# Spreading a row of 1/sigma over the partitions: three products with the identity in place of a round trip through DRAM

## The chip, the cores and the metric

The kernel runs on one core of one Trainium2 chip. The metric is the device time of one execution in microseconds (us). A core has five engines, each with its own instruction queue that is worked off in order: TensorE (PE in the profile; its weight loads stand apart as PEld), VectorE (DVE), ScalarE (ACT), GpSimd (POOL) and SyncE (SP), which here only issues transfers. ACT and POOL issue transfers too; a queue's own issuing instructions are marked SPq and ACTq.

## The reference

Three parts follow each other. Attention over short windows gives x of shape 4 x 768 x 512. A Fourier mixer adds to x the real part of its two-dimensional Fourier transform, normalises each position, applies a two-layer network and adds the result. A gated convolutional network ends it.

```python
u = x + real(fft(fft(x, axis=1), axis=2))
mu = mean(u, axis=-1); var = mean((u - mu) ** 2, axis=-1)
un = (u - mu) / sqrt(var + 1e-06)
x2 = u + maximum(un @ w_ch1, 0) @ w_ch2          # 512 -> 2048 -> 512
h = maximum(x2 @ w_in, 0)                        # 512 -> 1024
...
out = (h * sigmoid(conv(h)) @ w_out)
```

## The kernel before

Positions lie along the free dimension and features on the partitions. The 4 x 768 positions are cut into 8 chunks of 384 (`TC`); chunk c is half of batch c // 2. Each fp32 number is held as a high and a low part in the type fp32r, and a product of two of them is three matmuls (`split3`, recorded on line 65 by `accumulate`).

The mixer's network is computed on u - mu without the division. Since relu(a x) = a relu(x) for positive a, the factor 1/sigma of a position may be multiplied in at the end. That is what the tile `rb` is for: it holds the 384 values of 1/sigma of one chunk on each of the 128 partitions.

The network has 16 tiles f of 128 hidden features. The first 4 are done early, in `dense`. The rest is done in 13 steps s, which one loop walks through. A step is one chunk with a run of tiles f: steps 0 to 4 take tiles 4 to 8 of chunks 0 to 4, steps 5 to 9 take tiles 9 to 15 of the same chunks (7 tiles), steps 10 to 12 take tiles 4 to 15 of chunks 5 to 7 (12 tiles). The eight steps from 5 on are the last of their chunk, and each of these runs `prep_stat` once. For each tile the loop calls:

- `g1`: 12 matmuls into the PSUM tile `h`; ACT makes `hh` of it (line 477) and DVE `hl` (line 478);
- one piece of `prep_stat`, up to its next `yield`, as long as there is one;
- `g2`: 12 matmuls of an earlier tile into four accumulators `acc`. At the last tile of a step `finish` follows: DVE adds `acc` to `yp` (line 709), multiplies by `rb` (line 715), and POOL's queue adds the result into `ucd` in DRAM (line 716). This comes in the first tile of the next step.

The pieces of `prep_stat`, with the tile j of the step in which each is called: j = 0, ACT squares u (line 662) and POOL's queue adds the mean into DRAM; j = 1, DVE sums the squares into `sq` (lines 666 and 667); j = 2, nothing; j = 3, PE sums over the partitions into `pvar` (line 672: three fp32 matmuls with one column, which the profile counts as six), and DVE and ACT read it into `st`; j = 4, DVE makes 1/sigma in `st` (lines 678 to 682), as 128 partitions x 3 values; j = 5, ACT's queue writes those 384 values to `rd` in DRAM (line 684); j = 6, SP's queue reads the row back, once for each partition, into `rb` (line 687).

The order of the work on each engine is that of the code. PSUM tiles `h`, `pvar` and whatever else is tagged "g" take turns in three buffers here. The same loop runs the decoding of the weights of the last part (tiles `w`, `wsc`, `wlb`, `whb`, `wo`, `wihd`) on ACT, DVE and SP's queue, in pieces.

Of the kernel before, what the change touches and what calls it, by code (L numbers as in the profile page):

```python
# [7 lines left out]
F32 = mybir.dt.float32  # L8
# [8 lines left out]
NB, NH, S, HD = 4, 8, 768, 64  # L17
# [8 lines left out]
TC = 384  # L26
# [19 lines left out]
def fourier_mixer_kernel(ctx: ExitStack, tc: tile.TileContext, qk, vw, w1, w2, w_in, w_out, conv_w,  # L46
                         mask, ident, dtab, orow, stab, sgn, out):
    nc = tc.nc
    mm = nc.tensor.matmul

    dram = ctx.enter_context(tc.tile_pool(name="dram", bufs=1, space=DRAM))
# [15 lines left out]
    const = ctx.enter_context(tc.tile_pool(name="const", bufs=1))  # L67
# [5 lines left out]
    nc.vector.memset(expb, -float(EXP0 << 23))  # L73
    expl = const.tile([128, 1], F32, name="expl")
    nc.vector.memset(expl, -float(896 << 23))
    stg = ctx.enter_context(tc.tile_pool(name="stg", bufs=2))
    rx = ctx.enter_context(tc.tile_pool(name="rx", bufs=1, side="right"))
    a1p = tc.alloc_tile_pool(name="a1p", bufs=2)
    ps_g = tc.alloc_tile_pool(name="ps_g", bufs=PSG, space=PSUM)
# [3 lines left out]
    order = []  # L83
    for f in range(NI, NF1):
        order += [("1", f), ("2", f)]
    rd = [dram.tile([1, TC], F32, name=f"rd{c}") for c in range(2 * NB)]
    wihd = [dram.tile([128, 1024], F32, name=f"wihd{f}") for f in range(NF2)]
    wohd = [dram.tile([128, 1024], F32, name=f"wohd{f}") for f in range(NF2)]

# [88 lines left out]
    for nm, dst in (("a", w1h), ("b", w1l), ("c", w2h), ("d", w2l)):  # L178
        t = rx.tile([128, 512 * NI], F32R, tag=f"rx{nm}", name=f"rx{nm}")
# [8 lines left out]
    cst = tc.alloc_tile_pool(name="cst", bufs=1)  # L188
# [5 lines left out]
    ps_o = tc.alloc_tile_pool(name="ps_o", bufs=1, space=PSUM)  # L194

    mask_sb = cst.tile([QB, 3, KW], F32, name="mask_sb")
    ident_sb = cst.tile([128, 128], F32, name="ident_sb")
    dtab_sb = cst.tile([128, 2, 2, CW + SW], F32R, name="dtab_sb")
    orow_sb = cst.tile([1, CW], F32R, name="orow_sb")
    stab_sb = cst.tile([97, 2, 8, 194], F32R, name="stab_sb")  # L200
# [367 lines left out]
    with tc.manual_schedule():  # L568
# [44 lines left out]
        ps_g = tc.alloc_tile_pool(name="ps_g2", bufs=3, space=PSUM, reuse_waits="tile")  # L613
        uc1 = tc.alloc_tile_pool(name="uc1", bufs=1, reuse_waits="tile")
        NC1 = NB * S // TC
        NTC = TC // 128
# [5 lines left out]
        def half(c):  # L622
            b, hf = divmod(c, 2)
            return b, slice(hf * TC, hf * TC + TC)
# [30 lines left out]
        def prep_stat(s):  # L655

            d = ck[s]
            c = steps[s][0]
            b, ss = half(c)
            sq = uc1.tile([128, 4, TC], F32, tag="sq", name="sq")  # L660
            for j in (0, 2):
                nc.scalar.activation(out=sq[:, j:j + 2], in_=d["us"][:, j:j + 2], func=AF.Square)
            nc.gpsimd.dma_start(out=ucd[b][:, :, ss], accum_op=ALU.add,
                                in_=mud[b][:, ss].rearrange("o (k t) -> o k t", k=1).to_broadcast([128, 4, TC]))
            yield
            nc.vector.tensor_tensor(out=sq[:, 0:2], in0=sq[:, 0:2], in1=sq[:, 2:4], op=ALU.add)  # L666
            nc.vector.tensor_tensor(out=sq[:, 0], in0=sq[:, 0], in1=sq[:, 1], op=ALU.add)
            yield
            yield
            p = ps_g.tile([128, 512], F32, tag="g", name="pvar")  # L670
            for t in range(NTC):
                mm(p[:, t:t + 1], sq[:, 0, t * 128:t * 128 + 128], onesm[:, 0:1], start=True, stop=True)  # L672
            st = uc1.tile([128, 4, NTC], F32, tag="st", name="st", bufs=2)
            ve, sd, r, e = (st[:, i] for i in range(4))
            nc.vector.tensor_scalar(out=ve, in0=p[:, 0:NTC], scalar1=0.5, scalar2=1e-6, op0=ALU.mult, op1=ALU.add)
            nc.scalar.activation(out=sd, in_=p[:, 0:NTC], func=AF.Sqrt, bias=epsc[:, 0:1], scale=0.5)
            yield
            nc.vector.reciprocal(out=r, in_=sd)
            nc.vector.tensor_tensor(out=e, in0=r, in1=r, op=ALU.mult)
            nc.vector.tensor_tensor(out=e, in0=e, in1=ve, op=ALU.mult)  # L680
            nc.vector.tensor_scalar(out=e, in0=e, scalar1=-0.5, scalar2=1.5, op0=ALU.mult, op1=ALU.add)
            nc.vector.tensor_tensor(out=r, in0=r, in1=e, op=ALU.mult)
            yield
            nc.scalar.dma_start(out=rd[c].rearrange("o (t p) -> p (o t)", p=128), in_=r)
            d["r"] = a1p.tile([128, TC], F32, tag="y", name="rb")
            yield
            nc.sync.dma_start(out=d["r"], in_=rd[c].to_broadcast([128, TC]))

        def g2(s, f):
            d = ck[s]  # L690
# [40 lines left out]
        for i, (s, f) in enumerate(seq):  # L731
            c, fs, last = steps[s]
# [9 lines left out]
            if j == 0 and last:  # L742
                stat = prep_stat(s)
# [106 lines left out]
    with tc.manual_schedule():  # L850
# [21 lines left out]
        for i in range(len(steps) + LAG):  # L872
# [5 lines left out]
            if i < len(steps):  # L878
                b, f = steps[i]
# [132 lines left out]
```

## Time and profile before

| | |
|---|---|
| time, median of 3 runs (lowest to highest) | 1075.61 us (1075.1 to 1075.64) |
| the profiled execution's own time | 1073.26 us |
| its span, first to last instruction | 1071.5 us |
| PE busy | 1024.6 us (96%) |
| DVE busy | 662.2 us (62%) |
| ACT busy | 431.4 us (40%) |
| mean granted clock of PE | 0.973 |
| steps 5 to 12 of the loop, about | 470 to 796 us of the span |

The profiled execution lies 2.35 us under the median, and the span 1.76 us under that execution's own time. A busy PE counts its time at any clock, so 96% isn't the share in which it works at its full rate; the granted clock says how far the rate fell.

### The profile page before, as it was taken

The numbers are of one execution on the slowest core, as the hardware profiler recorded it, in microseconds if no ns is written. First come the engines' busy times: TensorE is split into PE (matmuls) and PEld (weight loads), VectorE is DVE, ScalarE is ACT, GpSimd is POOL, SyncE is SP. The second block draws the span as 40 slices with busy tenths as digits, with TensorE's granted clock in tenths as the row PEclk, the third lists the DMA queues.
The fourth block names the chain that finished last, engine by engine and source line by source line (L and its number), as shares of the span: only waits on it lengthen the run. The fifth ranks groups of instructions, "written<-read, shape, count | busy, mean of one in ns | idle before, by whom it ended". The sixth has DMA issues, their size and how long they took to land.

```text
span 1071.5 us, 16522 instructions
## 1 busy us (share of the span) xinstructions
PE 1024.6 (96%) x6352; PEld 974.1 (91%) x6352; DVE 662.2 (62%) x1505; ACT 431.4 (40%) x894; POOL 229.9 (21%) x236
## 2 busy tenths in 40 slices
PE   6879999899998999999989998999999999999998
PEld 5769998799998999999989998999998999999997
DVE  5897659865989666664654544342337656566554
ACT  6855446653343433233322231222126445454442
POOL 2353343652513000010000000000202322222222
PEclk9877999899999999999989998999999999999999
DMA  7841433520435544587798689461945302010001
GB/s 248 281 137 56 144 106 107 178 56 31 141 108 192 197 152 153 200 187 129 183 206 173 115 157 193 120 96 37 207 111 139 103 12 82 26 59 1 33 27 60
DMA packets 68127, 132.44 MB, mean 124 GB/s; under 512 B 8215, under 2 KB 43519, under 8 KB 67823
## 3 DMA queue, kind: packets, MB, share of 16 engines
q1 hardware_dynamic: 52576, 103.93, 31.6%
q0 software_dynamic: 12016, 27.16, 14.4%
q10 hardware_dynamic: 3456, 0.29, 0.3%
q8 instruction: 50, 0.82, 0.3%
q14 instruction: 29, 0.24, 0.1%
HBM read 93.85 MB, written 43.80 MB: 128 GB/s over the span
## 4 chain that ended last, share of the span: by engine, by line
PE 57%; DMA 8%; DVE 4%; issue 1%; ACT 0%; POOL 0%; DVEq 0%; ACTq 0%; POOLq 0%; SPq 0%
PE acc L65 27%; PE h L65 16%; PE ph L65 11%; DMA rd<-st 5%; DMA rb<-rd 2%; PE y L65 2%; DVE yp L715 1%; DMA wot<-wohd 1%; PE pvar L672 1%; DMA ucd<-uc 0%; DVE wsc L135 0%; DVE sq L666 0%; DVE hl L478 0%; DVE whb L131 0%; DVE uc L165 0%
## 5 line engine op out<-in xcount | busy, mean ns | idle before, releaser
L65 PE MATMUL acc<-hh,w 128*128 128x384 f32 x768 | 214.7, 343 | 0.0
L65 PE MATMUL h<-uh,w 128*128 128x384 f32 x768 | 212.0, 340 | 0.0
L478 DVE SCALAR_TENSOR_TENSOR hl<-h,hh 128x384 fp32r<-128x384 f32 x128 | 70.6, 555 | 190.1 <-ACT hh L477 189.1
L477 ACT ACTIVATE hh<-h 128x384 fp32r<-128x384 f32 x128 | 61.9, 488 | 234.0 <-PE h L65 233.9
L65 PEld LDWEIGHTS acc<-hh,w 128*128 128x128 f32 x768 | 143.7, 192 | 0.0
L65 PEld LDWEIGHTS h<-uh,w 128*128 128x128 f32 x768 | 142.7, 191 | 0.0
L65 PE MATMUL ph<-xh,wit 128*128 128x384 f32 x512 | 136.3, 337 | 2.2 <-ACT hrow L802 2.2
L65 PE MATMUL acc<-hl,w 128*128 128x384 f32 x384 | 131.6, 343 | 0.0
L65 PE MATMUL h<-ul,w 128*128 128x384 f32 x384 | 130.4, 340 | 0.0
L65 PE MATMUL acc<-wot,hgh 128*128 128x512 f32 x384 | 119.7, 393 | 0.0
L810 DVE SCALAR_TENSOR_TENSOR cv<-hrow,cw_sb,cv 128x768 f32<-128x768 f32 x64 | 110.1, 1720 | 3.1 <-ACT cv L804 2.0
L822 POOL TENSOR_TENSOR hgl<-cv,hgh 128x768 fp32r<-128x768 f32 x32 | 60.3, 1883 | 196.1 <-ACT hgh L821 180.5
L65 PEld LDWEIGHTS ph<-xh,wit 128*128 128x128 f32 x512 | 93.3, 188 | 4.0 <-ACT hrow L802 2.8
L816 DVE TENSOR_TENSOR cv<-hrow,cv 128x768 f32<-128x768 f32 x32 | 30.7, 960 | 99.0 <-ACT cv L815 98.9
L65 PE MATMUL ph<-xl,wit 128*128 128x384 f32 x256 | 86.1, 336 | 0.0
L65 PEld LDWEIGHTS acc<-wot,hgh 128*128 128x128 f32 x384 | 71.7, 188 | 13.4
L241 ACT ACTIVATE sm<-sm,ngm 96x128 f32<-96x128 f32 x256 | 80.0, 392 | 7.7 <-DVE ngm L233 7.7
L65 PE MATMUL acc<-wot,hgl 128*128 128x512 f32 x192 | 74.7, 389 | 0.0
L65 PEld LDWEIGHTS acc<-hl,w 128*128 128x128 f32 x384 | 73.7, 192 | 0.0
L65 PEld LDWEIGHTS h<-ul,w 128*128 128x128 f32 x384 | 73.3, 191 | 0.0
L802 ACT ACTIVATE hrow<-ph 128x384 f32<-128x384 f32 x64 | 31.2, 493 | 102.2 <-PE ph L65 101.1
L716 POOL DMA_DIRECT2D ucd<-yp x8 | 9.7, 1208 | 286.3 <-DVE yp L715 194.4
(142 smaller groups left out, 1912.1 us busy)
## 6 DMA issues: line engine op xcount, KB each, us to landing
w<-in_w SPq DMA_DIRECT2D x32, 512.0 KB, 4.1
qk<-in_qk SPq DMA_DIRECT2D x32, 448.0 KB, 3.6
us<-ucd SPq DMA_DIRECT2D x13, 768.0 KB, 7.3
yp<-yd SPq DMA_DIRECT2D x13, 768.0 KB, 7.9
vw<-in_vw SPq DMA_DIRECT2D x32, 260.0 KB, 2.7
ucd<-uc SPq DMA_DIRECT2D x8, 768.0 KB, 3.8
yd<-y SPq DMA_DIRECT2D x32, 192.0 KB, 1.9
ucd<-mud POOLq DMA_DIRECT2D x8, 768.0 KB, 20.2
```

Of the source, the lines that this page charges most:

```text
L65: mm(o, a, b, start=(start and i == 0), stop=(stop and i == n - 1))
L241: nc.scalar.activation(out=d["ex"][:, h, :], in_=d["ex"][:, h, :], func=AF.Exp, scale=-1.0, bias=d["ngm"][:, h:h + 1])
L477: nc.scalar.activation(out=hh, in_=p[:, 0:TC], func=AF.Relu)
L478: nc.vector.scalar_tensor_tensor(out=hl, in0=p[:, 0:TC], scalar=0.0, in1=hh.bitcast(F32), op0=ALU.max, op1=ALU.subtract)
L672: mm(p[:, t:t + 1], sq[:, 0, t * 128:t * 128 + 128], onesm[:, 0:1], start=True, stop=True)
L715: nc.vector.tensor_tensor(out=y[:, t:t + 2], in0=y[:, t:t + 2], in1=bc, op=ALU.mult)
L716: nc.gpsimd.dma_start(out=ucd[b][:, :, ss], in_=y, accum_op=ALU.add)
L802: nc.scalar.activation(out=h[:, 1 + hf * TC:1 + hf * TC + TC], in_=p[:, 0:TC], func=AF.Relu)
L810: nc.vector.scalar_tensor_tensor(out=cv, in0=h[:, j:j + S], scalar=cw_sb[:, j, f:f + 1], in1=cv, op0=ALU.mult, op1=ALU.add)
L816: nc.vector.tensor_tensor(out=cv, in0=h[:, 1:S + 1], in1=cv, op=ALU.mult)
L822: nc.gpsimd.tensor_tensor(out=hgl[i], in0=cv, in1=hgh[i].bitcast(F32), op=ALU.subtract)
```

## The change

The row no longer goes to DRAM. At j = 5 PE makes three products, one for each 128 positions: the weights are one column of 1/sigma, repeated 128 times, and the moving operand is the 128 x 128 identity, so that each of the 128 partitions of the result gets the 128 values. ACT copies the result from PSUM into `rb`. The write to `rd` (ACT's queue), the read (SP's queue) and the piece at j = 6 go. The identity, which only the attention part used before, moves into a pool that lives to the end. That takes 512 bytes of each partition, and what lies behind it in SBUF moves up by as much.

```diff
+    ident_sb = const.tile([128, 128], F32, name="ident_sb")
...
-    rd = [dram.tile([1, TC], F32, name=f"rd{c}") for c in range(2 * NB)]
...
-    ident_sb = cst.tile([128, 128], F32, name="ident_sb")
...
             nc.vector.tensor_tensor(out=r, in0=r, in1=e, op=ALU.mult)
             yield
-            nc.scalar.dma_start(out=rd[c].rearrange("o (t p) -> p (o t)", p=128), in_=r)
+            p = ps_g.tile([128, 512], F32, tag="g", name="prow")
+            for t in range(NTC):
+                mm(p[:, t * 128:t * 128 + 128], r[:, t:t + 1].to_broadcast([128, 128]), ident_sb, start=True, stop=True)
             d["r"] = a1p.tile([128, TC], F32, tag="y", name="rb")
-            yield
-            nc.sync.dma_start(out=d["r"], in_=rd[c].to_broadcast([128, TC]))
+            nc.scalar.copy(d["r"], p[:, 0:TC])
```

On PE, at j = 5 of step 6 (chunk 1), these rows stood between the products of `h` and of `acc` before (the numbers behind the names are buffers):

```order
L65 MATMUL h<-uh,w_14_4389 128x384 x2
L65 MATMUL h<-ul,w_14_4389 128x384
L65 MATMUL h<-uh,w_14_4389 128x384
L65 MATMUL acc<-hh,w_12_4386 128x384 [waits Activation_49]
L65 MATMUL acc<-hl,w_12_4386 128x384
L65 MATMUL acc<-hh,w_12_4386 128x384 x2
```

and these now:

```order
L65 MATMUL h<-uh,w_14_4381 128x384 x2
L65 MATMUL h<-ul,w_14_4381 128x384
L65 MATMUL h<-uh,w_14_4381 128x384
L685 MATMUL prow<-ident_sb,st 128x128 [waits DVE_49,Activation_49]
L685 MATMUL prow<-ident_sb,st 128x128 x2
L65 MATMUL acc<-hh,w_12_4378 128x384
L65 MATMUL acc<-hl,w_12_4378 128x384
```

Three products came in, and the first waits for DVE (the values) and for ACT (the PSUM buffer, and with it `hh`, for which `acc` waited before).

On ACT, in the same place, the queue held before:

```order
L477 ACTIVATE hh<-h 128x384 [waits PE_49,Activation_49] x2
L684 DMA rd_93<-st 128x3x1 [waits DMAHW2_49,DVE_49]
L162 CAST uh<-us 128x768 [waits DMAHW5_49]
L162 CAST uh<-us 128x768
L134 COPY wo<-whb 128x512 [waits DMAHW3_49,DVE_49]
```

and now:

```order
L476 ACTIVATE hh<-h 128x384 [waits PE_49,Activation_49] x2
L687 COPY rb<-prow 128x384 [waits PE_49]
L162 CAST uh<-us 128x768 [waits DMAHW3_49]
L162 CAST uh<-us 128x768
L134 COPY wo<-whb 128x512 [waits DMAHW1_49,DVE_49]
```

A copy that waits for PE stands where the write was issued. On SP, at j = 6 of the same step, one issue before left between a spill of decoded weights and a fetch of the next; before:

```order
L144 DMA wihd_103<-wo 128x512 [waits DMAHW1_49,DVE_49]
L687 DMA rb<-rd_93 128x384 [waits DMAHW3_49,DMAHW2_49]
L94 DMA w_6224<-in_w_in 128x512 [waits DMAHW4_49,DVE_49]
L143 DMA wihd_104<-wo 128x512 [waits DMAHW5_49,Activation_49]
L144 DMA wihd_104<-wo 128x512 [waits DMAHW6_49,DVE_49]
L630 DMA us<-ucd_58 128x4x384 [waits DMAHW7_49]
```

and now:

```order
L144 DMA wihd_96<-wo 128x512 [waits DMAHW7_49,DVE_49]
L94 DMA w_6222<-in_w_in 128x512 [waits DMAHW0_49,DVE_49]
L143 DMA wihd_97<-wo 128x512 [waits DMAHW1_49,Activation_49]
L144 DMA wihd_97<-wo 128x512 [waits DMAHW2_49,DVE_49]
L629 DMA us<-ucd_58 128x4x384 [waits DMAHW3_49]
```

Here the read of the row, which waited for its own write, is gone, and nothing else has moved. On the other queues the order of the instructions is the same as before.

## Rows read from the trace of the kernel before

**Rows 1.** The page, busy time: us, share of the span, instructions.

```profile
PE 1024.6 (96%) x6352; PEld 974.1 (91%) x6352; DVE 662.2 (62%) x1505; ACT 431.4 (40%) x894; POOL 229.9 (21%) x236
```

**Rows 2.** Who PE waited for, 300 to 830 us: us in total, times, longest.

```profile
PE pvar L672 <- DVE sq L667: 10.5, 4, 4.1
```

**Rows 3.** PE's `pvar` products in time: start, us, engine, line [idle before].

```profile
482.75 0.72 PE L672 MATMUL pvar<-onesm,sq 128*128 128x1 f32 x6
...
513.13 0.74 PEld L672 LDWEIGHTS pvar<-onesm,sq 128*128 128x128 f32 x6 [0.29 <-DVE sq L667]
...
546.35 1.44 PE L672 MATMUL pvar<-onesm,sq 128*128 128x1 f32 x6 [2.72 <-DVE sq L667]
...
582.04 0.83 PE L672 MATMUL pvar<-onesm,sq 128*128 128x1 f32 x6 [2.25 <-DVE sq L667]
...
615.49 0.83 PE L672 MATMUL pvar<-onesm,sq 128*128 128x1 f32 x6 [1.48 <-DVE sq L667]
...
651.47 1.18 PE L672 MATMUL pvar<-onesm,sq 128*128 128x1 f32 x6 [4.09 <-DVE sq L667]
...
705.86 0.72 PE L672 MATMUL pvar<-onesm,sq 128*128 128x1 f32 x6
...
756.99 0.72 PE L672 MATMUL pvar<-onesm,sq 128*128 128x1 f32 x6
```

**Rows 4.** Stretches: span, busy of PE, PEld, DVE, ACT, POOL, PEclk, DMA share, GB/s.

```profile
480.00:513.00 33.00, 33.00 (x191) 32.83 (x189) 18.78 (x39) 11.49 (x19) 1.21 (x1) 1.00 0.81 179
...
546.00:582.00 36.00, 33.44 (x174) 33.12 (x174) 17.48 (x37) 9.00 (x16) 3.42 (x3) 0.91 0.89 166
...
706.00:757.00 51.00, 51.00 (x296) 51.00 (x295) 14.35 (x28) 9.08 (x17) 2.87 (x4) 1.00 0.37 61
```

**Rows 5.** DVE in time, from the end of step 6 on.

```profile
534.17 1.94 DVE L709 TENSOR_TENSOR yp<-acc,yp 128x384 f32<-128x384 f32 x4
541.34 1.83 DVE L715 TENSOR_TENSOR yp<-yp,rb 128x768 f32<-128x768 f32 x2 [5.24 <-DMA rb<-rd]
...
544.29 0.55 DVE L478 SCALAR_TENSOR_TENSOR hl<-h,hh 128x384 fp32r<-128x384 f32 x1
544.76 0.94 DVE L666 TENSOR_TENSOR sq<-sq 128x768 f32<-128x768 f32 x1
545.74 0.56 DVE L667 TENSOR_TENSOR sq<-sq 128x384 f32<-128x384 f32 x1
```

**Rows 6.** Who DVE waited for: us in total, times, longest.

```profile
DVE yp L715 <- DMA rb<-rd: 25.6, 5, 7.4
```

**Rows 7.** The row's way in step 6: last DVE instruction, write and read issued.

```profile
520.19 0.16 DVE L682 TENSOR_TENSOR st<-st 128x3 f32<-128x3 f32 x1
...
522.69 0.37 ACTq L684 DMA_DIRECT2D rd<-st  x1
...
536.14 0.32 SPq L687 DMA_DIRECT2D rb<-rd  x1
```

**Rows 8.** PE in time: an fp32 product of 384 columns, and what follows.

```profile
315.98 0.81 PE L410 MATMUL pm<-gs,onesm 128*128 128x384 f32 x2
316.33 0.66 PE L65 MATMUL p<-stab_sb,zh 96*128 96x194 f32 x2
316.83 0.27 PE L65 MATMUL p<-stab_sb,zl 96*128 96x194 f32 x1
316.94 0.39 PE L65 MATMUL p<-stab_sb,zh 96*128 96x194 f32 x2
```

**Rows 9.** PE in time, behind the `pvar` of 705.86.

```profile
706.44 0.42 PE L65 MATMUL acc<-hh,w 128*128 128x384 f32 x1
706.70 0.34 PE L65 MATMUL acc<-hl,w 128*128 128x384 f32 x1
706.88 0.51 PE L65 MATMUL acc<-hh,w 128*128 128x384 f32 x2
```

**Rows 10.** ACT: a copy of 128 x 384 from PSUM.

```profile
20.21 0.48 ACT L162 COPY at<-atp 128x384 f32<-128x384 f32 x1 [0.23 <-PE atp L250]
```

## Prediction

> **What bounds the kernel now.** The page's busy table comes first: PE is busy for 1024.6 us of a span of 1071.5 [rows 1]. So PE is the path, and a change elsewhere pays only where it ends one of PE's waits or takes work from it. The list of who waited for whom, cut to 300 to 830 us (the loop over the 13 steps), shows one wait that counts: `pvar`, for the sum of squares `sq` from DVE [rows 2]. The same products in order of time show where: five of the eight `pvar` come late, with idle times of 0.29, 2.72, 2.25, 1.48 and 4.09 us, together 10.83 us [rows 3]. (The list counts four of them and a little less, since PE's weight load waits apart.)
>
> Idle time is not the whole price. A stretch without a stall, 706 to 757 us, has a granted clock of 1.00; the one that holds the end of one stall and the beginning of the next, 546 to 582 us, has 0.91 [rows 4]. So PE falls from the upper level of 2.4 GHz to the lower one, 1.2 GHz, for some microseconds after a stall. The whole price can be read from the distances between the starts of `pvar`, since the work between them is fixed: seven tiles up to step 10, twelve after it. Without a stall twelve tiles take 756.99 - 705.86 = 51.13 us. Seven take 513.13 - 482.75 = 30.38 us, of which 0.29 is idle, so 30.09. (The two fit: five tiles more cost 21.04 us, 4.21 each.) The others, start to start, are 33.22, 35.69, 33.45, 35.98 and, with twelve tiles, 54.39 us [rows 3]. Over the unstalled length they lose 3.13, 5.60, 3.36, 5.89 and 3.26 us; with the first 0.29 that is **21.5 us**, about half idle and half lower clock.
>
> Why is `sq` late? DVE's timeline at the end of step 6 shows it. DVE has added the accumulators by 536.1 us and then stands still for 5.24 us, until `rb` has landed; only then come the multiplication, some decoding, `hl` and the two sums into `sq`, which end at 546.3 [rows 5]. PE starts `pvar` at 546.35 [rows 3]. Over the whole run DVE waited five times for `rb`, 25.6 us in all [rows 6], once for each stall. And `rb` is late because of its way: 1/sigma is there at about 520.4, the write is issued at 522.69, and the read, which waits for the write, only at 536.14 [rows 7].
>
> **What the change takes away.** Everything between 522.7 us and the landing before 541.34 goes. The products stand where the write was issued, so in this step `rb` would be ready about 1.5 us after 522.5 us, and DVE asks for it at 536.1: 12 us of cover. Then the multiplication and all behind it come 5.24 us earlier, and `sq` is ready 5.24 - 2.72 = 2.5 us before PE asks. At the longest wait it is 7.4 - 4.09 = 3.3 us, and over the five (25.6 - 10.83) / 5 = 3.0 us on average. So each of the five stalls should go whole, and with it the fall of the clock behind it, since it needs the stall. Next in line for PE would be `hl`, which the same queue delivers, also 5 us earlier. I take the full 21.5 us; the lower end is given by the second rival.
>
> A rule in the Trainium skill speaks against this: the page DMA: Bandwidth & Descriptors (section Anatomy of one DMA, SWDGE path) puts the fixed cost of a transfer at about 2 us. By it the row would be written and back about 4.5 us after 522.69 (an estimate: twice 2 us and 0.45 us for 197 KB), at 527.2, long before DVE asks, and the change would take away nothing. The trace differs: between the two issues alone lie 13.45 us [rows 7]. The measurement decides; what it leaves of that case is the fourth rival.
>
> **What it adds on PE.** Eight times three fp32 products of 128 columns, six passes in the profile's count, as `pvar` has. No row shows this form, so it is bounded. From below: `pvar` itself, six loads of 128 x 128 weights with one column each. From its start at 705.86 to the next product 0.58 us pass, 0.097 a pass, all of it weight load; the first product behind takes 0.26 instead of 0.18 [rows 3, 9]. So the detour costs 0.66 us, and eight cost 5.3 us. The columns: the fp32 product `pm` with 384 columns and the two short products behind it take 0.85 us from 315.98 to 316.83; the short ones take 0.11 each [rows 8], which leaves 0.63 for two passes and, by thirds, 0.105 us for 128 columns. If loads lie under the columns of the pass before, as `pvar`'s neighbours do, a pass costs the larger of the two: 6 x 0.105 + 0.08 = 0.71. I take **0.75**, in all **6.0 us**. From above: if nothing overlaps, 6 x 0.202 + 0.08 = 1.29, in all 10.3 us. That the weights are one column read 128 times has no row at all; I leave it inside these bounds, which would still hold a load twice as long.
>
> The page TensorE: Matmul & The Clock Gate (section LDWEIGHTS) makes a load as long as its columns, 107 ns for 128. The trace has 97 ns for it. By the page's figure a detour would be 6 x 0.107 + 0.08 = 0.72 us (an estimate), 5.8 us in all.
>
> The first of the new products waits for DVE's 1/sigma and for a PSUM buffer. The values end at 520.35, and ACT's issue behind `hh`, which marks the end of `h` on PE, stands at 522.69 [rows 7]: a slack of about 2.2 us. The seven other steps repeat this pair within 0.4 us. The buffer was `pvar`'s, read two tiles before.
>
> **What it moves.** ACT loses an issue of 0.37 us and gains a copy of about 0.48 [rows 7, 10]. Behind it the two casts of `uh` wait for it, and behind those `hh` of the next tile, whose products end 4.2 us and a detour later; ACT is busy for 9.00 of 36 us there [rows 4]. It costs nothing; without that cover it would be 8 x 0.5 us. SP's queue no longer stands before the read, so fetches, `us` and `yp` go out earlier; they are wanted many microseconds later. The transfer engines are busy for 0.81 of a stretch that PE runs through without a stall, and 0.89 of a stalled one [rows 4]. With the steps shorter, the same bytes come in less time, but 8 x 197 KB of reads go. The 512 bytes that shift later tiles change which old tile a new one waits for; those waits are for work done long before. Both at nothing.
>
> **The sum.** -21.5 + 6.0 = -15.5 us. On the profiled execution's own time, 1073.26, that gives 1057.8. The median of the runs shown is 2.35 us above it; on 1075.61 it gives **1060.1 us**.
>
> **The rivals.**
> 1. *The products are dear.* Loads of a repeated column don't overlap with the columns, or are slower. Against it: weight loads and matmuls are both busy nearly all the time in the same stretches [rows 4]. -21.5 + 10.3 = -11.2, 1064.4 us.
> 2. *Another wait takes the place of the one removed.* With the row out of the way, DVE is held by something else in the same place, say a fetch of weights in transfer engines that are fuller, so that `sq` still comes late in about half the cases. For it: 0.89 of DMA share. Against it: 2.5 to 3.3 us of margin. -10.8 + 6.0 = -4.8, 1070.8 us.
> 3. *Slower: PE waits for 1/sigma.* The new products stand in PE's queue, in front of `acc`; the DMA waited elsewhere. If DVE delivers the values more than 2.2 us later than now, PE stalls in eight places instead of five. The stalls of 1.48 to 4.09 us cost 3.1 to 5.9 with the clock. It decides from (21.5 - 6.0) / 8 = 1.9 us for each place; at 3 us each the kernel is 8.5 us slower, 1084.1. Against it: DVE makes these values right behind `hl`, and a DVE that waits less is earlier, not later.
> 4. *Nothing is gained.* `rb` has long landed, and DVE's wait is only put down to it and ends with something else; then only the products are left, +6.0, 1081.6 us. Against it: the five waits of rows 6 and the read's issue 5.2 us before the end of the one shown [rows 5, 7]. (This is where the rule of DMA: Bandwidth & Descriptors in the Trainium skill leads.)
>
> That the change doesn't do what it says is no rival: the order of the instructions shows the products on PE and no transfer.
>
> **Chances and range.** The forecast 0.74, dear products 0.12, a new wait 0.08, PE waits for 1/sigma 0.04, nothing gained 0.02. About 0.2% (2.1 us) is what a measurement of this kernel can tell from no change. The first three are faster, less 0.01 for a new wait that eats nearly all: faster 0.93, same 0.02 (with as much from a milder third rival), slower 0.05. The range: the cheapest products give 1075.6 - 21.5 + 5.3 = 1059.4, and as the runs shown lie up to 2.4 us beside the profiled one, 1057.0; the dearest give 1064.4, and with 2.4 us again 1066.8. The rivals beyond it hold 0.14.
>
> **What the profile after would show.** DVE's wait for `rb` gone, and line 715's multiplication right behind the additions. No idle time before `pvar`, starts 30.8 us apart over seven tiles (30.09 and a detour of 0.75) and 51.9 over twelve, with a granted clock of 1.00 from 480 to 790 us. Six passes of `prow` in 0.6 to 0.8 us, eight times, without idle time before them. The forecast is wrong if `pvar` still waits, if `prow` waits for DVE, or if its passes take 0.2 us each.

## The result and the profile after

The changed kernel takes **1060.8 us** (median of 4 runs, 1059.1 to 1064.62) against 1075.62 us before (4 runs, 1075.1 to 1076.58): a ratio of **0.9866, interval 0.9839 to 0.9894**. The profiled execution took 1059.1 us with a span of 1057.3; before it was 1073.26 and 1071.5. The medians here take in every execution, while the ratios and intervals are of the means and leave out the few executions that ran more than 1.5% over the fastest of their kernel.

The page's busy times of the changed kernel come first, beside [rows 1]:

```profile
PE 1023.2 (97%) x6400; PEld 974.5 (92%) x6400; DVE 662.5 (63%) x1505; ACT 435.4 (41%) x902; POOL 230.0 (22%) x236
```

PE has 48 instructions more, eight times six passes, and was still busy for no longer. Between the first and the last `pvar` it was busy for 263.75 us before, at a granted clock of 0.96, and for 258.00 us now, at 1.00: matmuls that no longer ran at the lower clock gave back more than the passes took. ACT's eight more are the copies. The list of who PE waited for, from 300 to 830 us, beside [rows 2] (us in total, times, longest), is now:

```profile
PE ph L65 <- ACT hrow L802: 2.2, 2, 1.8
PE h L65 <- DVE y L160: 1.6, 1, 1.6
PE y L65 <- DVE hl L477: 1.3, 2, 0.8
```

`pvar`, with 10.5 us the largest before, is not in it. The eight `pvar` products in order of time, beside [rows 3] (start, us), have no idle time in brackets any more:

```profile
484.51 0.72 PE L671 MATMUL pvar<-onesm,sq 128*128 128x1 f32 x6
515.41 0.72 PE L671 MATMUL pvar<-onesm,sq 128*128 128x1 f32 x6
546.31 0.72 PE L671 MATMUL pvar<-onesm,sq 128*128 128x1 f32 x6
...
638.86 0.72 PE L671 MATMUL pvar<-onesm,sq 128*128 128x1 f32 x6
690.69 0.72 PE L671 MATMUL pvar<-onesm,sq 128*128 128x1 f32 x6
742.49 0.72 PE L671 MATMUL pvar<-onesm,sq 128*128 128x1 f32 x6
```

They are 30.90 us apart over seven tiles (30.74 up to step 10) and 51.8 over twelve; 30.8 and 51.9 were predicted. The first lies 1.76 us later than before, and the span behind the last is 0.3 us longer, so the whole difference of the spans (14.2 us) and a little more arises between the first and the last: 274.24 us before, 257.98 now, 16.26 less.

The stretches, beside [rows 4] (span, busy of PE, PEld, DVE, ACT, POOL, granted clock, DMA share, GB/s):

```profile
480.00:790.00 310.00, 309.64 (x1799) 309.32 (x1798) 146.62 (x298) 84.32 (x152) 22.46 (x27) 1.00 0.64 149
546.00:577.00 31.00, 31.00 (x182) 31.00 (x181) 17.29 (x36) 9.48 (x17) 2.42 (x2) 1.00 0.87 177
```

The clock is 1.00 over the whole loop, and PE is busy without a gap. DVE in order of time at the end of step 6 shows what [rows 5] showed:

```profile
537.01 1.94 DVE L709 TENSOR_TENSOR yp<-acc,yp 128x384 f32<-128x384 f32 x4
538.87 1.82 DVE L715 TENSOR_TENSOR yp<-yp,rb 128x768 f32<-128x768 f32 x2
...
542.27 0.95 DVE L665 TENSOR_TENSOR sq<-sq 128x768 f32<-128x768 f32 x1
543.26 0.56 DVE L666 TENSOR_TENSOR sq<-sq 128x384 f32<-128x384 f32 x1
```

The multiplication stands right behind the additions. `sq` ends at 543.82, and PE asks for it at 546.31: 2.5 us of margin. Of the row's own way, the last DVE instruction on 1/sigma [rows 7] and the copy that replaced the transfers [rows 10] are these, in order of time:

```profile
522.36 0.16 DVE L681 TENSOR_TENSOR st<-st 128x3 f32<-128x3 f32 x1
...
525.39 0.48 ACT L687 COPY rb<-prow 128x384 f32<-128x384 f32 x1
```

And PE's products between them, with their neighbours, beside [rows 8, 9]:

```profile
524.52 0.83 PE L685 MATMUL prow<-ident_sb,st 128*128 128x128 f32 x6
525.11 0.42 PE L65 MATMUL acc<-hh,w 128*128 128x384 f32 x1
525.37 0.34 PE L65 MATMUL acc<-hl,w 128*128 128x384 f32 x1
525.54 0.52 PE L65 MATMUL acc<-hh,w 128*128 128x384 f32 x2
```

`rb` is there at 525.9, 13 us before DVE uses it. The six passes hold the next product back by 0.59 us, and the one behind starts after 0.26 instead of 0.18: a detour of 0.67 us, which is `pvar`'s 0.66 [rows 3, 9]. Divided by six, 0.59 us is 0.098 a pass, but that is not a pass's own length: taken one by one, the passes start 0.11 us apart (524.52, 524.63, 524.74, 524.86, 524.97, 525.08), and only behind the last one the next product follows after 0.03.

### The profile page after: what moved, and what is told of

It is laid out like the page before. It is cut to its first block, busy times and chain, and to the rows that moved or that the text cites. A ratio compares the mean times of both kernels' runs of the same rounds, so it can differ in the third digit from the quotient of the medians.

```text
span 1057.3 us, 16601 instructions
## 1 busy us (share of the span) xinstructions
PE 1023.2 (97%) x6400; PEld 974.5 (92%) x6400; DVE 662.5 (63%) x1505; ACT 435.4 (41%) x902; POOL 230.0 (22%) x236
## 4 chain that ended last, share of the span: by engine, by line
PE 65%; DVE 2%; DMA 1%; issue 0%; ACT 0%; POOL 0%; DVEq 0%; POOLq 0%; SPq 0%
PE acc L65 31%; PE h L65 20%; PE ph L65 12%; PE y L65 2%; DMA wot<-wohd 1%; PE prow L685 1%; PE pvar L671 0%; DMA ucd<-uc 0%; DVE wsc L135 0%; DVE uc L165 0%; DVE yp L709 0%; DMA out<-o 0%; DVE yp L715 0%; DVE hl L477 0%; DVE w L139 0%
## 5 line engine op out<-in xcount | busy, mean ns | idle before, releaser
L65 PE MATMUL acc<-hh,w 128*128 128x384 f32 x768 | 211.2, 338 | 0.0
L65 PE MATMUL h<-uh,w 128*128 128x384 f32 x768 | 209.7, 337 | 0.0
L65 PEld LDWEIGHTS acc<-hh,w 128*128 128x128 f32 x768 | 140.5, 188 | 0.0
L65 PEld LDWEIGHTS h<-uh,w 128*128 128x128 f32 x768 | 140.4, 188 | 0.0
L65 PE MATMUL acc<-hl,w 128*128 128x384 f32 x384 | 129.3, 337 | 0.0
```

Source lines behind the costliest of these rows:

```text
L65: mm(o, a, b, start=(start and i == 0), stop=(stop and i == n - 1))
```

## The experiments

The theory: the kernel before lost its time because DVE stood at line 715, in front of `sq`, waiting for a row on its way through DRAM, and the products cost what six passes cost. The first rival: the transfers themselves (their share of queues and engines, or of the layout) were the cost. The second: the products take over the role of the wait.

Whole times of one kernel spread by 2 to 4 us either way, and the traces place that spread in the first 300 us, where the granted clock is 0.91 to 0.94 from run to run (at the sixth step's `pvar` one execution stands at 513 us and another at 526). So beside the medians each run is read by its **stretch**, from the sixth step's `pvar` to the twelfth's (steps 6 and 12 of the loop): six distances. Before it is 756.99 - 513.13 = 243.86 us [rows 3]; in the changed kernel 742.49 - 515.41 = 227.08.

### The change again, on another chip

The changed kernel, with no edit.

> The changed kernel once more, to measure beside the others. Both theories: 1060.8 us as in the four runs so far, between 1059 and 1065; 14 to 16 us under the kernel before.

1061.15 us (6 runs) against 1072.92, ratio 0.9887, interval 0.9864 to 0.9909. The stretch is 227.08 us, to the hundredth that of the first chip. What differs is the kernel before: 1072.92 us here, 1075.62 there, so the gain is 11.8 us and not the expected 14 to 16. The gain is real; its size hangs on the kernel before (below).

### The wait moved off DVE's queue, the transfers kept

On the kernel before, the multiplication and the transfer behind it are put off to the third tile of the next step, behind `sq` (`scale` holds the four lines that are taken out above it, and runs once more after the last step):

```diff
-            bc = d["r"].rearrange("p (o t) -> p o t", o=1).to_broadcast([128, 2, TC])
-            for t in (0, 2):
-                nc.vector.tensor_tensor(out=y[:, t:t + 2], in0=y[:, t:t + 2], in1=bc, op=ALU.mult)
-            nc.gpsimd.dma_start(out=ucd[b][:, :, ss], in_=y, accum_op=ALU.add)
+            scaled.append((d, b, ss))
+
+        scaled = []
+
+        def scale():
+            while scaled:
+                d, b, ss = scaled.pop(0)
...
             if j == 2:
+                scale()
                 prep_y(s)
```

> The kernel before, row by way of DRAM, but the multiplication by rb and its transfer wait until the third tile (j = 2) of the next step, so that in DVE's queue the sums into sq stand ahead of it. Theory (the gain is DVE's wait in front of sq): all five stalls of 21.5 us go and no product is added, 1054 us, faster than the changed kernel by 5 to 6; no idle time before pvar. Rival (the gain comes from the transfers that are gone, by fuller DMA engines or by SP's queue standing before the read): the transfers are all there, so 1075 us. Third way: the wait for rb now holds hl of the tile behind it, and PE stalls there: between 1060 and 1075, with idle time before acc.

1059.44 us (6 runs), ratio 0.9874, interval 0.9844 to 0.9904, and a stretch of 737.97 - 514.90 = 223.07 us. The median lies 5 us over the expected 1054; the profiled execution took 1054.82 us. DVE in order of time at the end of step 6 of this kernel:

```profile
540.07 0.95 DVE L666 TENSOR_TENSOR sq<-sq 128x768 f32<-128x768 f32 x1
541.05 0.56 DVE L667 TENSOR_TENSOR sq<-sq 128x384 f32<-128x384 f32 x1
541.86 0.55 DVE L478 SCALAR_TENSOR_TENSOR hl<-h,hh 128x384 fp32r<-128x384 f32 x1
543.46 1.83 DVE L723 TENSOR_TENSOR yp<-yp,rb 128x768 f32<-128x768 f32 x2 [1.05 <-DMA rb<-rd]
```

Its waits for `rb` over the whole run (us in total, times, longest), and the `pvar` of the next two steps on PE:

```profile
DVE yp L723 <- DMA rb<-rd: 11.3, 4, 5.0
```

```profile
545.15 0.72 PE L672 MATMUL pvar<-onesm,sq 128*128 128x1 f32 x6
575.39 0.72 PE L672 MATMUL pvar<-onesm,sq 128*128 128x1 f32 x6
```

DVE still waits 11.3 us for the row, but with nothing urgent behind it: `pvar` has no idle time, and seven tiles take 30.24 us. PE's one idle time for `hl`, the third way that was put down, is 0.32 us at 773 us, behind the last `pvar`. All of the stalls are gone with every transfer still in place, so what cost the time was the place of the wait in DVE's queue. The first rival falls. The stretch is also 4.01 us shorter than the changed kernel's, six detours of 0.67: this is the loop with neither stalls nor products.

### The transfers kept beside the products

The changed kernel, with the write and the read issued too, into a tile that nobody reads:

```diff
+    rd = [dram.tile([1, TC], F32, name=f"rd{c}") for c in range(2 * NB)]
...
             nc.scalar.copy(d["r"], p[:, 0:TC])
+            nc.scalar.dma_start(out=rd[c].rearrange("o (t p) -> p (o t)", p=128), in_=r)
+            yield
+            rx2 = uc1.tile([128, TC], F32, tag="rbx", name="rbx")
+            nc.sync.dma_start(out=rx2, in_=rd[c].to_broadcast([128, TC]))
```

> The changed kernel, and beside the products the write to DRAM and the read back stay, into a tile that nobody reads. Theory: nobody waits for them, so 1060.8 us within 1 us. Rival (transfers or SP's queue were the cost): the gain of 14.8 us goes in large part, 1068 to 1076 us.

1061.66 us (6 runs), ratio 0.9903, interval 0.9877 to 0.9929; the stretch 748.56 - 521.48 = 227.08, exactly that of the change. The bytes, the issue on ACT and the read in SP's queue cost nothing in the loop.

### The identity moved alone

The kernel before, with the identity's tile put where the change puts it:

```diff
+    ident_sb = const.tile([128, 128], F32, name="ident_sb")
...
-    ident_sb = cst.tile([128, 128], F32, name="ident_sb")
```

> The kernel before with only the identity moved to the pool that lives to the end, so that later tiles shift by 512 bytes and wait for other old tiles. Theory: no change, as the kernel before within what its runs differ by (1070 to 1077 us), and 243.9 us from the sixth to the twelfth step's pvar. Rival (part of the gain is the new layout): some us faster.

1067.98 us (12 runs) against 1067.15, ratio 1.0022, interval 1.0002 to 1.0042: the shift of later tiles gives nothing. DVE waits for `rb` five times here too, 18.8 us in all. The expected 1070 to 1077 us and the stretch of 243.9 us were missed: the stretch is 749.35 - 514.80 = 234.55 us. Both figures came from other chips. That the kernel before has a stretch like this on the present one is inferred from the two medians; no trace of it was taken there.

### The products twice

```diff
-            for t in range(NTC):
+            for t in (*range(NTC), *range(NTC)):
```

> The changed kernel with each product of the row made twice into the same place, so 48 fp32 products in place of 24. Theory (the passes lie on PE's path at the 0.098 us that they have in the trace, load-bound): 8 x 6 x 0.098 = 4.7 us more, 1065.5 us. If the dear bound held, 8 x 6 x 0.2 = 9.7 us more, 1070.5. If the products fill time in which PE would have waited anyway, no change, 1060.8.

1064.52 us (12 runs), ratio 0.9929, interval 0.9905 to 0.9953; 3.4 us over the change on the same chip, where 4.7 were expected. PE in order of time shows the doubled group:

```profile
534.69 1.50 PE L685 MATMUL prow<-ident_sb,st 128*128 128x128 f32 x12
535.94 0.42 PE L65 MATMUL acc<-hh,w 128*128 128x384 f32 x1
```

1.25 us for twelve passes, again 0.11 us from start to start, and a stretch of 756.53 - 525.57 = 230.96, which is 3.88 more than the change, 0.65 for each extra six. So the eight cost 5.2 to 5.4 us, read three ways (neighbours, doubled, and left out above). They are not dear, but six more passes cost 0.65 us and not the 0.59 of six times 0.098.

### The products one tile earlier

The changed kernel without the `yield` ahead of the products, so that PE reaches them a tile sooner than DVE has 1/sigma: the prediction's third rival, made real by moving the products and not the values.

```diff
             nc.vector.tensor_tensor(out=r, in0=r, in1=e, op=ALU.mult)
-            yield
             p = ps_g.tile([128, 512], F32, tag="g", name="prow")
```

> The changed kernel with the products at j = 4, right behind the last DVE instruction of 1/sigma in place of a tile later, so that PE reaches them about 2.2 us before the values are there. Nothing on DVE or in the queues waits for more. Theory (each stall of PE costs its idle time and a spell at the lower clock): eight stalls of about 2.2 us at the 4.1 us that the stall of 2.25 us cost before, 33 us more than the changed kernel, about 1094 us; from the sixth to the twelfth step's pvar 227.1 + 6 x 4.1 = 251.7 us. Rival (the idle time is all that a stall costs): 8 x 2.2 = 18 us more, about 1079, and 240.3 us. If PE doesn't wait there: 1061.

1085.52 us (6 runs) against 1067.15, ratio **1.019, interval 1.0159 to 1.0222**: slower than before. PE's waits show why (us in total, times, longest):

```profile
PE prow L684 <- DVE st L681: 16.9, 8, 2.1
```

Eight equal stalls of 2.11 us. Their price is not equal. PE in order of time at the second and the third:

```profile
524.82 1.65 PE L684 MATMUL prow<-ident_sb,st 128*128 128x128 f32 x6 [2.11 <-DVE st L681]
526.13 0.67 PE L65 MATMUL acc<-hh,w 128*128 128x384 f32 x1
...
559.64 0.93 PE L684 MATMUL prow<-ident_sb,st 128*128 128x128 f32 x6 [2.11 <-DVE st L681]
560.34 0.42 PE L65 MATMUL acc<-hh,w 128*128 128x384 f32 x1
```

And the stretches from step to step, with the granted clock in the third place from the end:

```profile
517.70:552.50 34.80, 32.69 (x182) 32.37 (x181) 17.18 (x35) 9.36 (x17) 2.41 (x2) 0.95 0.65 154
552.50:585.80 33.30, 31.19 (x183) 30.87 (x181) 17.27 (x35) 9.49 (x17) 2.42 (x2) 1.00 0.68 165
585.80:620.50 34.70, 32.59 (x181) 32.27 (x180) 18.05 (x36) 10.19 (x18) 2.42 (x2) 0.95 0.64 128
620.50:653.70 33.20, 31.09 (x184) 30.77 (x182) 17.19 (x36) 9.46 (x17) 2.42 (x2) 1.00 0.80 174
```

After the second stall the six passes take 1.31 us from start to start, at a granted clock of 0.50, the lower level (1.2 GHz); after the third they take 0.70, at 1.00. Over the 30.9 us of the changed kernel the steps shown lose 3.9 and 2.4 us in turn. Of the eight stalls the first, second, fourth and sixth were followed by a fall of the clock, and their steps lost 3.9 to 4.3 us; behind the four others none is seen. The stretch is 763.62 - 517.66 = 245.96, 18.88 over the change, 3.15 a stall, between the 2.11 of the idle time alone and the price of a stall with its fall of the clock each time. Both expectations missed.

### The write issued earlier

The kernel before without the `yield` ahead of the write, so that the write leaves a tile earlier and the read too stands a tile earlier in SP's queue:

```diff
-            yield
             nc.scalar.dma_start(out=rd[c].rearrange("o (t p) -> p (o t)", p=128), in_=r)
```

> The kernel before, row by way of DRAM, with the write at j = 4, right behind the last DVE instruction of 1/sigma, and the read at j = 5. The write goes out about 2.3 us earlier, so DVE waits 2.3 us less each time. Theory: the idle times of 0.29, 2.72, 2.25, 1.48 and 4.09 us fall to 0, 0.4, 0, 0 and 1.8, and the cost of the five stalls from 21.5 to about 5 us; the time is 15 to 18 us under the kernel before, and from the sixth to the twelfth step's pvar 226 to 229 us in place of 243.9. Rival (the stalls come from the transfers being there, not from when they land): as the kernel before.

1064.31 us (12 runs), ratio 0.9969, interval 0.9944 to 0.9995: little. The stretch is 746.59 - 515.06 = 231.53 us, outside the expected 226 to 229, and 3.0 us under that of the kernel with the identity moved. DVE's five waits were to be 2.3 us shorter each; they are 2.49, 2.08, 4.34, 7.67 and 2.60, 19.2 us in all, as the 18.8 of the kernel with the identity moved, on the same chip. One row's issues in this kernel, after a `pvar` at 545.30:

```profile
552.45 0.37 ACTq L683 DMA_DIRECT2D rd<-st  x1
```

```profile
567.75 0.32 SPq L686 DMA_DIRECT2D rb<-rd  x1
```

and in the kernel with the identity moved, after a `pvar` at 545.04:

```profile
554.49 0.37 ACTq L684 DMA_DIRECT2D rd<-st  x1
```

```profile
569.07 0.32 SPq L687 DMA_DIRECT2D rb<-rd  x1
```

The write leaves 7.15 us after `pvar` instead of 9.45, but the read, which waits for it, only 22.45 instead of 24.03 after. Over the five rows for which DVE waited, the time between the two issues is 14.7 us on average here and 12.3 there: what the early issue gained was lost in flight. The expectation failed, and why the write took longer stays open. (It also reckoned with the 21.5 us of the first chip; against the unstalled 223.07 us the kernel with the identity moved had only 11.5 to lose in the stretch.) In the first trace of the kernel before, a part of the 13.45 us of one row, 528.7 to 535 us, has the transfer engines nearly idle:

```profile
528.70:535.00 6.30, 6.30 (x37) 6.30 (x36) 1.92 (x5) 1.83 (x3) 0.00 (x0) 1.00 0.02 1
```

A DMA share of 0.02 says that large transfers don't fill the engines there; whether the write waits, or is itself moved so slowly, no row shows.

### Before, after and the late multiplication on further chips

The late multiplication again beside the two kernels above, on their chip; then the kernel before, the changed one and the late multiplication together on another.

> The late multiplication by way of DRAM once more, since the six runs of the first time lay 7 us apart. By the traces its loop is 5.4 us shorter than the changed kernel's for want of the products; so 5 us under the changed kernel's 1061 us in the median, 1056 us, and 223.1 us from the sixth to the twelfth step's pvar.

> The kernel before itself, with a trace, beside the two others on one chip, since its time differed between the chips so far (1075.6, 1072.9 and 1067.2 us). Theory (only its waits for the row differ): the idle time before a pvar is DVE's wait for rb less about 3.0 us, and none under that; from the sixth to the twelfth step's pvar it takes 223.1 us and what these stalls cost, between 230 and 245. Rival (the chips differ in something else): that stretch differs in the two other kernels too.

> The changed kernel on the same chip. Theory: 227.1 us from the sixth to the twelfth step's pvar, whichever chip it is, about 1061 us in all, so that the gain is as large as the kernel before's stalls on this chip, less 5.4 us for the products: 6 to 16 us. Rival: the stretch is another one here.

> The late multiplication by way of DRAM on the same chip: 223.1 us for that stretch and a median 4 to 6 us under the changed kernel's.

| kernel, chip | us, median | before there | ratio, interval | stretch, us |
|---|---|---|---|---|
| changed, first | 1060.8 | 1075.62 | 0.9866, 0.9839 to 0.9894 | 227.08 |
| changed, second | 1061.15 | 1072.92 | 0.9887, 0.9864 to 0.9909 | 227.08 |
| late multiplication, second | 1059.44 | 1072.92 | 0.9874, 0.9844 to 0.9904 | 223.07 |
| late multiplication, third | 1056.53 | 1067.15 | 0.9910, 0.9886 to 0.9934 | 223.07 |
| before, fourth | 1073.77 | 1074.09 | 1.0002, 0.9980 to 1.0024 | 240.52 |
| changed, fourth | 1060.55 | 1074.09 | 0.9875, 0.9848 to 0.9903 | 227.08 |
| late multiplication, fourth | 1057.57 | 1074.09 | 0.9870, 0.9822 to 0.9918 | 223.07 |

The changed kernel's stretch is the same on the three chips on which it ran, and so is that of the late multiplication, though DVE's waits for the row came to 11.3, 0.5 and 12.0 us in its three traces. The expectations of these runs held, but for the last median: 3.0 us under the changed kernel's, where 4 to 6 were expected. The kernel before has 243.86, 240.52 and (with the identity moved) 234.55, and in the traces the part of it that varies is the landing of the row. Four executions with their five waits each show how the wait turns into a stall (DVE's wait for `rb`, then PE's idle time before `pvar`, us; the first trace's longest wait is 7.36):

| execution | DVE's waits | PE's idle times |
|---|---|---|
| before, first chip | 3.09, 5.24, 5.37, 4.56, 7.36 | 0.29, 2.72, 2.25, 1.48, 4.09 |
| before, fourth chip | 3.40, 4.60, 3.92, 7.11, 5.01 | 0.29, 2.10, 0.81, 3.99, 1.76 |
| identity moved | 1.64, 1.69, 5.62, 3.06, 6.78 | 0, 0, 2.52, 0.27, 3.53 |
| write earlier | 2.49, 2.08, 4.34, 7.67, 2.60 | 0, 0, 1.23, 4.56, 0 |

PE idles for DVE's wait less about 3 us (2.5 to 3.3), and not at all where the wait is shorter. So the margin of 2.5 to 3.3 us that the prediction worked out for `sq` is also the cover that the kernel before had, and its loss moves with the landing: with 18.8 us in the five waits instead of 25.6 its stretch is 11.5 us over the unstalled 223.07 and not 20.8.

## Why the prediction was right

- **The bound and the wait.** Confirmed. Moving DVE's wait from in front of `sq` to behind it, with nothing else taken away, ended all the stalls, and a row waited for elsewhere is harmless.
- **The stalls go whole.** Confirmed, with the margin worked out for step 6 (2.5 us) found to the tenth, and the clock at 1.00 from 480 to 790 us. The price of the stalls was slightly oversized: against the late multiplication, whose first and last `pvar` lie 737.97 - 484.67 = 253.30 us apart, the kernel before lost 274.24 - 253.30 = 20.9 us, not 21.5, since an unstalled seven tiles take 30.23 to 30.25 us in four places of five (30.08 in the last) and not 30.09.
- **The products.** 0.67 us a detour, 5.4 in all, not 0.75 and 6.0. The value at the bottom, `pvar`'s own 0.66, was the right one: passes of 128 columns start 0.11 us apart, as those of `pvar` with its one column do, so the columns add nothing to the load. A repeated column as weights costs no more. The 0.097 us that the prediction gives for a pass, and the 97 ns for a load, were misread: from 705.86 to the next product lie five distances of 0.11 and one of 0.03, and `pvar`'s loads start 0.11 us apart too. The whole detour of 0.66 doesn't hang on that division. The two terms were off by the same 0.6 us in opposite directions, so -20.9 + 5.4 gives the predicted -15.5, and that it fits to the tenth is luck; the medians of the first chip show -14.8.
- **The slack of 1/sigma.** The values end at 522.52, and PE comes to the products at 524.52: 2.0 us, for the 2.2 predicted, and no wait in eight places. One tile earlier it is -2.11 and the kernel is slower than before, so this was the edge that mattered.
- **ACT, SP's queue, the layout.** At nothing each, as put down: the stretch is six detours over the unstalled one and no more, which leaves nothing for ACT's copy; the kept transfers and the moved identity show the rest.
- **The rivals.** Dear products fall by the doubled ones. For another wait, the DMA share of the steps was 0.34 to 0.87, and in the loop nothing took DVE's place. That nothing is gained falls by every run of the changed kernel.
- **The sizes left.** What the prediction didn't see is that the gain belongs to the chip: 14.8, 11.8 and 13.5 us by the medians where the changed kernel ran. On the third chip the changed kernel wasn't run; 234.55 - 227.08 = 7.5 us of its stretch would be the gain there, less two further products, an inference. And "the fall of the clock needs the stall" holds, but a stall doesn't always bring it: of eight equal ones four did.

The late multiplication beats the changed kernel by 4.01 us in the stretch, and from the first `pvar` to the end of the span by 6.0 us on the second chip and 5.0 on the fourth (eight detours are 5.4); the medians differ by 1.7 us on the second chip and 3.0 on the fourth, within their spread, so the stretch carries this verdict, not the medians. Against the kernel before it is faster on three chips.

## What to carry to other kernels

Where an engine in order waits for something slow, first look at what stands behind the waiting instruction and who waits for that: putting the instruction behind the urgent work may end the stall for nothing, where replacing the slow source costs work on the bounding engine. Price a stall by the distance between fixed marks of the waiting engine, not by its idle time, which was about half of it in the kernel before and two thirds with the products a tile early. And when such work is moved onto the bounding engine, its place in the order is worth more than its own cost: one tile earlier it was a loss of 1.9%, and no longer a gain of 1.1 to 1.3% (measured on other chips).

## What was not expected of the hardware

- Eight equal stalls of 2.11 us lowered the granted clock four times only: 0.95 to 0.97 over the steps where it fell, 1.00 over the others, at 3.9 to 4.3 and 2.0 to 2.4 us a step.
- A write of 1.5 KB into DRAM took 8 to 18 us until the read that waits for it was issued (in the four executions of the table of waits), in part with the transfer engines at a share of 0.02, and issuing it 2.3 us earlier brought the read only 1.6 us forward in the step shown.
- The kernel before differed by 8.5 us between four chips (1067.15 to 1075.62); the changed one, with no landing in its path, by 0.6 between the three on which it ran.
